# Moving transposes of attention outputs and of late q from the tensor engine to the DMA, with v sorted earlier and k sorted per batch

## The chip, the cores and the metric

One core of one Trainium2 chip. The metric is the device time of one execution in microseconds (us). Executions of one kernel mostly agree within 0.3 to 1%; verdicts compare kernels run alternately on the same chip. A ratio below is the mean time of one kernel's fast runs over that of the other's fast runs of the same rounds, so it is not quite the ratio of the medians that stand beside it. An execution more than 1.5% above the fastest of the same kernel is labelled slow. Spans in a profile are some 2 us shorter than the device time. A profile is of one execution of a kernel, not of the median. To land, for a DMA, is counted from the start of its issue until its data is there.

PE is the tensor engine, ACT the scalar engine, DVE the vector engine, POOL the GpSimd engine, SP the sync engine, which here only issues DMAs.

## The reference

```
P = sort_net; 5 times: softmax over rows, then divide by the column sums     # 4 batches, 8 heads, 8x8
k_sorted = einsum('bhij,bhjcd->bhicd', P, k_b)      # 8 blocks of 96 rows, d = 64; v likewise
attn = softmax(q_b @ k_sb^T / 8) @ v_sb             # inside each block of 96
x = attn, as 3072 tokens x 512
g = s * relu(x @ w_in)^2 + b                        # 512 -> 2048
out = g @ w_out                                     # 2048 -> 512, float32
```

## The kernel before

All work is in eight tiles of 384 tokens; a batch is two tiles. A tile's attention (scores, exp on ACT, product with v, division on DVE) leaves `X[t]` with tokens on partitions. The first dense layer (`ffn1`) needs features on partitions (`XT[t]`), so PE transposes X into PSUM and an engine copies it out. The pieces of later tiles' attention are slotted between the matmuls of the dense layers by queues: q of a batch is transposed by PE, k and v are sorted by PE with block-diagonal matrices `pd1` (batches 0, 1) and `pd2` (batches 2, 3).

```
    def q_piece(b, hp0, eng):                     # q: 24 PE transposes and a copy of 128x1536
        ...
    def k_piece(b, c0, nc2, nb, eng):             # k: nc2 matmuls, 4 copies out of PSUM
        ...
    def v_read(b, eng):                           # sorted v goes to DRAM and is read back,
        ...                                       # 64 values (128 bytes) to a row
            eng.dma_start(out=VS[b][cp * (BLK // 2):(cp + 1) * (BLK // 2), :, 0:D],
                          in_=src.rearrange("g (c two) d -> two c g d", two=2)[cp])
    def t_piece(t, eng, n0=0, nn=HB):             # x: 16 PE transposes and a copy
        ...
    ffn2(1, qu)
    v_read(3, nc.gpsimd)
    load_q(3)
    ...                                           # q and k of batch 2 in the queue
    ffn1(2, qu)
    ffn1(3, qu)
    qu = Queue(attn(4) + attn(5), 24)
    ffn2(2, qu)
    ffn2(3, qu)
```

PSUM buffers are `psa` (3 buffers of two banks, for the first layer and most pieces) and `psb` (2 of one bank, for the second layer). DMAs of one issuing engine are issued in program order; POOL issues the loads and the read-back of sorted v of batches 2 and 3, SP the stores.

The softmax here doesn't subtract the row's maximum and nothing guards it: scores larger than these inputs give would overflow.

## Time and profile before

The median is 249.4 us (248.31 to 249.7 over 4 runs). PE is the bound: 94% busy. The groups of PE work give a timeline by stage (a stage begins with its first dense matmul; a pair of tiles each):

| stage | starts at, us | length, us |
|---|---|---|
| set-up, attention, first layer of tiles 0 and 1 | 0 | 61.9 |
| second layer 0, 1 with attention of 2, 3 | 61.9 | 35.3 |
| first layer 2, 3 with q and k of batch 2 (and k of 3) | 97.2 | 28.8 |
| second layer 2, 3 with attention of 4, 5 | 126.0 | 27.0 |
| first layer 4, 5 (nothing else) | 153.0 | 20.8 |
| second layer 4, 5 with attention of 6, 7 | 173.8 | 28.4 |
| the rest | 202.2 | 45.6 |

The lines behind this table stand in the prediction. Read the fifth row as the pace PE can have, and the third as the place where a first layer costs 8 us more than that.

### The profile page before, as it was taken

To read this page: it belongs to the slowest core of one execution; us is meant where nothing else is said; L and a number is where in the kernel's file an instruction comes from. 1 tells how busy PE (TensorE), PEld (TensorE's weight loads), DVE (VectorE), ACT (ScalarE), POOL (GpSimd) and SP (SyncE) were. 2 spreads that over 40 slices of the span, in tenths; PEclk is the share of its full clock that TensorE was granted. 3 is DMA by queue.
4 is the path that set the end of the run, shared out by engine and by line. 5 is a ranking of instruction groups with operands and counts; after the bars stand their busy time and mean duration, and the time that the engine had idled before them with its cause. 6 is when DMAs were issued, how large, how long until landed. Compare 5 with 4: busy or idle time off the path is not lost.

```text
span 247.8 us, 4978 instructions
## 1 busy us (share of the span) xinstructions
PE 233.1 (94%) x2128; PEld 140.9 (57%) x2128; DVE 133.2 (54%) x260; ACT 116.3 (47%) x156; POOL 39.3 (16%) x51
## 2 busy tenths in 40 slices
PE   8879799799999899998899999999999999999993
PEld 4578699645554456655555555666555566664441
DVE  5776556899992545846675345444353444442221
ACT  6346566335358274477852342666341536661000
POOL 7720200497910027000000000000000000000000
PEclk9955579999999999999999999999999999999999
DMA  5999999999799929991001212000012120001122
GB/s 65 195 194 212 212 205 205 218 204 236 144 99 152 343 90 145 132 173 22 0 4 42 87 43 84 4 0 0 4 42 87 42 87 0 3 0 42 51 76 86
DMA packets 20214, 24.97 MB, mean 101 GB/s; under 512 B 7520, under 2 KB 14432, under 8 KB 19680
## 3 DMA queue, kind: packets, MB, share of 16 engines
q0 software_dynamic: 8400, 15.21, 35.8%
q1 hardware_dynamic: 11792, 9.45, 14.8%
q8 instruction: 16, 0.26, 0.5%
q14 instruction: 6, 0.05, 0.1%
HBM read 29.63 MB, written 8.65 MB: 155 GB/s over the span
## 4 chain that ended last, share of the span: by engine, by line
PE 69%; DVE 12%; DMA 9%; ACT 6%; issue 1%; SPq 0%; DVEq 0%
PE ops L459 29%; PE hps L433 27%; DMA vs<-dv 5%; PE pv L386 4%; DVE gt L438 3%; DMA dv<-vn 3%; ACT rt L437 3%; PE sc L359 3%; PE tr L414 2%; ACT ks L230 2%; PE tv L304 2%; DVE ks L228 2%; DVE qt L228 1%; PE tk L278 1%; DMA sn<-in_sort_net_dram 1%
## 5 line engine op out<-in xcount | busy, mean ns | idle before, releaser
L433 PE MATMUL hps<-xt,wi 128*128 128x384 bf16 (+1 forms) x576 | 89.2, 311 | 2.4 <-ACT ks L230 1.1
L459 PE MATMUL ops<-wo,gt 128*128 128x512 bf16 x384 | 90.5, 380 | 0.0
L433 PEld LDWEIGHTS <-wi 128*128 128x128 bf16 x576 | 54.3, 99 | 31.7 <-issue 4.1
L437 ACT ACTIVATE rt<-hps 128x768 bf16<-128x768 f32 (+1 forms) x72 | 53.2, 739 | 38.1 <-PE hps L433 34.1
L438 DVE TENSOR_TENSOR gt<-rt 128x768 bf16<-128x768 bf16 (+1 forms) x72 | 43.0, 601 | 43.2 <-ACT rt L437 42.8
L459 PEld LDWEIGHTS <-gt 128*128 128x128 bf16 x384 | 35.1, 98 | 38.4 <-issue 0.6
L450 DVE SCALAR_TENSOR_TENSOR ot<-ops,s_bc,bias 128x512 f32<-128x512 f32 x24 | 18.0, 748 | 36.4 <-PE ops L459 36.4
L362 ACT ACTIVATE at<-sc 96x768 bf16<-96x768 f32 x32 | 24.2, 802 | 24.1 <-PE sc L359 24.1
L391 DVE TENSOR_TENSOR x<-pv,rec 96x512 bf16<-96x512 f32 (+1 forms) x36 | 22.6, 628 | 1.3
L230 ACT COPY xt<-tr 128x1536 bf16<-128x1536 bf16 x6 | 8.6, 1438 | 23.6 <-PE tr L414 23.6
L228 DVE CAST ks<-tk 64x512 bf16<-64x512 f32 (+1 forms) x28 | 18.5, 662 | 1.7 <-PE tk L278 1.3
L583 POOL TENSOR_TENSOR csum<-csum,wo 128x512 f32<-128x512 f32 x14 | 17.6, 1255 | 1.0
L230 ACT CAST ks<-tk 64x512 bf16<-64x512 f32 (+1 forms) x24 | 13.9, 580 | 7.2 <-PE tk L278 6.9
L390 DVE RECIPROCAL rec<-pv 96x8 f32<-96x8 f32 (+1 forms) x36 | 7.0, 193 | 17.4 <-PE pv L386 17.4
L386 PEld LDWEIGHTS <-at 96*128 96x128 bf16 (+1 forms) x256 | 11.9, 104 | 5.6 <-DMA vs<-dv 1.5
L386 PE MATMUL pv<-vs,at 96*128 96x66 bf16 (+1 forms) x256 | 12.9, 199 | 1.8 <-DMA vs<-dv 1.0
L359 PEld LDWEIGHTS <-ks 64*96 64x96 bf16 x256 | 8.5, 132 | 6.1 <-issue 5.0
L359 PE MATMUL sc<-qt,ks 64*96 64x96 bf16 x256 | 10.8, 223 | 0.3 <-DVE ks L228 0.2
L172 PE MATMUL wp<-zt 128*128 128x256 bf16 x50 | 9.6, 321 | 1.1 <-DVE warm L104 1.1
L278 PE MATMUL tk<-pd,kb 64*128 64x64 bf16 (+1 forms) x144 | 8.3, 216 | 0.9 <-DVE pd L511 0.9
L278 PEld LDWEIGHTS <-kb 64*128 64x128 bf16 (+1 forms) x144 | 7.4, 106 | 3.0 <-issue 2.2
L228 DVE COPY qt<-tq 128x1536 bf16<-128x1536 bf16 x4 | 7.0, 1754 | 3.5 <-PE tq L259 3.5
(67 smaller groups left out, 116.8 us busy)
## 6 DMA issues: line engine op xcount, KB each, us to landing
out_dram<-ot SPq DMA_DIRECT2D x24, 256.0 KB, 2.0
kb<-in_k_dram POOLq DMA_DIRECT2D x4, 768.0 KB, 21.8
vb<-in_v_dram POOLq DMA_DIRECT2D x4, 768.0 KB, 19.0
qr<-in_q_dram POOLq DMA_DIRECT2D x3, 768.0 KB, 35.4
wi<-in_moe_w_in_dram POOLq DMA_DIRECT2D x2, 1024.0 KB, 19.1
wo<-in_moe_w_out_dram POOLq DMA_DIRECT2D x2, 1024.0 KB, 30.2
dv<-vn SPq DMA_DIRECT2D x6, 256.0 KB, 3.6
vs<-dv POOLq DMA_DIRECT2D x4, 384.0 KB, 11.3
```

Of the source, the lines that this page charges most:

```text
L228: nc.vector.tensor_copy(out=out, in_=in_)
L230: nc.scalar.copy(out=out, in_=in_)
L278: nc.tensor.matmul(out=ps[:, c, :], lhsT=kb[pr, c0 + 2 * c:c0 + 2 * c + 2, :].rearrange("p c d -> p (c d)"), rhs=rhs, start=True, stop=True)
L359: nc.tensor.matmul(out=sc[:, e, n * BLK:(n + 1) * BLK], lhsT=ks[pr, g0 + n, :], rhs=QT[b][pr, hp, q0:q0 + BLK], start=True, stop=True)
L362: nc.scalar.activation(out=at, in_=sc[:, :, 0:TG], func=AF.Exp, scale=scale)
L386: nc.tensor.matmul(out=pv[e][0:m, (n - n0) * VW:(n - n0 + 1) * VW], lhsT=atf[:, c0:c0 + m], rhs=VS[b][:, gi, :], start=True, stop=True)
L391: nc.vector.tensor_tensor(out=x[:, n0:n0 + nn, hp * 128:(hp + 1) * 128].rearrange("p n (e d) -> p e n d", e=2), in0=pvv[:, :, :, 0:D], in1 ...
L433: nc.tensor.matmul(out=hps[:, f, 0:nt], lhsT=wi_at(hp, f0 + f), rhs=xt[:, hp, c0:c0 + nt], start=(hp == 0), stop=(hp == NHP - 1))
L437: nc.scalar.activation(out=rt[:, :, 0:nt], in_=hps[:, :, 0:nt], func=AF.Relu)
L438: nc.vector.tensor_tensor(out=gt[:, f0:f0 + 2, c0:c0 + nt], in0=rt[:, :, 0:nt], in1=rt[:, :, 0:nt], op=ALU.mult)
L450: nc.vector.scalar_tensor_tensor(out=ot, in0=ops, scalar=s_bc, in1=bias, op0=ALU.mult, op1=ALU.add)
L459: nc.tensor.matmul(out=ops, lhsT=gt[:, f, m * 128:(m + 1) * 128], rhs=wo_at(f), start=(f == 0), stop=(f == NF - 1))
```

## The change

It wants PE free of transposes that a DMA can do, frees the copies out of PSUM that went with them, sorts v of batch 1 a stage earlier so that its way through DRAM is over in time, splits the k sort so that each piece is small, and moves the loads of k and q to where the queues reach them.

```diff
-    qtp = ctx.enter_context(tc.tile_pool(name="qtp", bufs=1))
+    qtp = ctx.enter_context(tc.tile_pool(name="qtp", bufs=2))
 ... q of batches 2, 3 loaded as six DMAs of rows of 64 values
+    def q_turn(b):
+        QT[b] = qtp.tile([128, NHP, S], BF, tag="qt", name=f"qt{b}")
+        for t in range(TQ):
+            nc.sync.dma_start(out=QT[b][:, :, t * 128:(t + 1) * 128],
+                              in_=qr[b][:, t].rearrange("p h d -> p (h d)"), transpose=True)
+    def x_turn(t):
+        XT[t] = xtp.tile([128, HB * NHP, BLK], BF, tag="xt", name="xt")
+        nc.sync.dma_start(out=XT[t], in_=X[t].rearrange("p n m -> p (n m)"), transpose=True)
     def T(t):
-        return lambda: t_piece(t, "s")
+        return lambda: x_turn(t)
 ... V1 (v of batch 1) moved from ffn1(1) into ffn1(0); load_k(2), load_q(2) moved from there
 ... to the queue of ffn2(0), with load_k(3)
-                  T(2), P2(3, 0), S2(3, 2), nothing, P2(3, 2), nothing, T(3)], 24)
+                  T(2), P2(3, 0), S2(3, 2), lambda: q_turn(2), P2(3, 2), T(3), nothing], 24)
-    pieces = [lambda: q_piece(2, 0, "v"), lambda: q_piece(2, 2, "v")]
-    for i in range(6):
-        pieces += K2(i * 16, "sv"[i % 2])
-    qu = Queue(pieces + [nothing], 16)
+    qu = Queue([nothing if i % 2 else K(2, i * 8, 8, "vs"[i // 2 % 2]) for i in range(12)]
+               + [nothing] * 4, 16)
     ffn1(2, qu)
     ffn1(3, qu)
+    v_read(3, nc.gpsimd)
+    load_q(3)
 ... K(3) in three pieces in the queue of ffn2(2); q_turn(3) after ffn2(3)
```

The order on SP that this makes: x of tile 2, six transposes of q of batch 2, then x of tile 3.

More of the change, by code (lines that the diff above doesn't have):

```diff
@@ L78, in load_q @@
     def load_q(b, part=slice(0, 128)):
+        if b > 1:
+            qr[b] = qrp.tile([128, TQ, H, D], BF, tag="qr", name=f"qr{b}")
+            for t in range(TQ):
+                nc.gpsimd.dma_start(
+                    out=qr[b][:, t],
+                    in_=q[b][:, t * 128:(t + 1) * 128, :].rearrange("h p d -> p h d"))
+            return
         if b not in qr:
@@ L263, in q_piece @@
              ps[:, :, 0:S].rearrange("q a (t p) -> q a p t", t=TQ), eng)
+    def q_turn(b):
+        QT[b] = qtp.tile([128, NHP, S], BF, tag="qt", name=f"qt{b}")
+        for t in range(TQ):
+            nc.sync.dma_start(out=QT[b][:, :, t * 128:(t + 1) * 128],
+                              in_=qr[b][:, t].rearrange("p h d -> p (h d)"), transpose=True)
     def k_piece(b, c0, nc2, nb, eng):
         pr = brows(b)[1] if nb == 1 else slice(0, 128)
-        rhs = (pd1[pr].rearrange("p e m i -> p (e m i)") if nb == 1
-               else pd2.rearrange("p b e m i -> p (b e m i)"))
+        rhs = (pd1[pr] if b < 2 else pd2[pr, b - 2]).rearrange("p e m i -> p (e m i)")
         if nc2 * nb > 8:
@@ L417, in t_piece, with xt_at @@
         evac(dst, src, eng)
+    def x_turn(t):
+        XT[t] = xtp.tile([128, HB * NHP, BLK], BF, tag="xt", name="xt")
+        nc.sync.dma_start(out=XT[t], in_=X[t].rearrange("p n m -> p (n m)"), transpose=True)
+    def xt_at(t, hp, n0, nn):
+        if t < 2:
+            return XT[t][:, hp, n0 * BLK:(n0 + nn) * BLK]
+        return XT[t].rearrange("p (n a) t -> p a n t", a=NHP)[:, hp, n0:n0 + nn, :]
     GT = {}
@@ L426, in ffn1 @@
             GT[t] = gtp.tile([128, NF, TG], BF, tag="gt", name="gt")
-        gt, xt = GT[t], XT[t]
+        gt = GT[t]
         c0, nt = n0 * BLK, nn * BLK
@@ L433, in ffn1 @@
                     nc.tensor.matmul(out=hps[:, f, 0:nt], lhsT=wi_at(hp, f0 + f),
-                                     rhs=xt[:, hp, c0:c0 + nt],
+                                     rhs=xt_at(t, hp, n0, nn),
                                      start=(hp == 0), stop=(hp == NHP - 1))
@@ L551 @@
     load_v(*brows(2))
-    load_k(*brows(2))
-    load_q(2)
     def P(t, hp, *r):
@@ L566 @@
                    lambda: t_piece(0, "v", 2, 2), SC(1, 3), P(1, 0)], 8), 0, 2)
-    ffn1(0, Queue([nothing, P(1, 1), nothing, P(1, 2), nothing, P(1, 3), nothing,
+    ffn1(0, Queue([V1(0), P(1, 1), V1(1), P(1, 2), V1(2), P(1, 3), V1(3),
                    lambda: t_piece(1, "v")], 8), 2, 2)
-    build_pd2()
-    V1(0)()
-    V1(1)()
+    V1(4)()
+    V1(5)()
     csum = const.tile([128, d_model], FP)
@@ L585 @@
     csums(0, 8)
-    ffn1(1, Queue([V1(i) for i in range(2, 6)] + [lambda: v_read(1, nc.sync)] + [nothing] * 3, 8))
+    v_read(1, nc.sync)
+    ffn1(1, Queue([nothing] * 4 + [build_pd2] + [nothing] * 3, 8))
     load_v(*brows(3))
@@ L592, with K @@
                + [lambda c0=c0: k_piece(1, c0, 16, 1, "vsv"[c0 // 32])() for c0 in range(0, BLK, 32)]
-               + [bias_piece, S2(2, 0), V2[0], S2(2, 2), V2[1], V2[2], V2[3],
+               + [seq(lambda: load_k(*brows(2)), lambda: load_k(*brows(3)), lambda: load_q(2), bias_piece), S2(2, 0), V2[0], S2(2, 2), V2[1], V2[2], V2[3],
                   P2(2, 0), V2[4], P2(2, 2), seq(V2[5], lambda: v_read(2, nc.gpsimd)), S2(3, 0),
-                  T(2), P2(3, 0), S2(3, 2), nothing, P2(3, 2), nothing, T(3)], 24)
+                  T(2), P2(3, 0), S2(3, 2), lambda: q_turn(2), P2(3, 2), T(3), nothing], 24)
     ffn2(0, qu)
-    load_k(*brows(3))
     ffn2(1, qu)
+    def K(b, c0, nc2, eng):
+        return lambda: k_piece(b, c0, nc2, 1, eng)()
+    qu = Queue([nothing if i % 2 else K(2, i * 8, 8, "vs"[i // 2 % 2]) for i in range(12)]
+               + [nothing] * 4, 16)
+    ffn1(2, qu)
+    ffn1(3, qu)
     v_read(3, nc.gpsimd)
     load_q(3)
-    rest = []
-    def K2(c0, eng):
-        return [lambda: rest.append(k_piece(2, c0, 8, 2, eng)), lambda: rest.pop()()]
-    pieces = [lambda: q_piece(2, 0, "v"), lambda: q_piece(2, 2, "v")]
-    for i in range(6):
-        pieces += K2(i * 16, "sv"[i % 2])
-    qu = Queue(pieces + [nothing], 16)
-    ffn1(2, qu)
-    ffn1(3, qu)
-    qu = Queue(attn(4) + attn(5), 24)
+    at4, at5 = attn(4), attn(5)
+    for i, n in enumerate((1, 4, 6)):
+        at4[n] = K(3, 32 * i, 16, "vsv"[i])
+    qu = Queue(at4 + at5, 24)
     ffn2(2, qu)
     ffn2(3, qu)
+    q_turn(3)
     ffn1(4)
     ffn1(5)
-    qu = Queue([lambda: q_piece(3, 0, "s"), lambda: q_piece(3, 2, "v")]
-               + attn(6) + attn(7), 24)
+    qu = Queue(attn(6) + attn(7), 24)
     ffn2(4, qu)
```

## The prediction

> **What bounds the kernel now.** I read the first part of the page first, for the busiest engine, then the summary of the chain that ended last, then a table of busy time by stage, and last the waits of the tensor engine (PE).
>
> ```profile
> PE 233.1 (94%) x2128; PEld 140.9 (57%) x2128; DVE 133.2 (54%) x260; ACT 116.3 (47%) x156; POOL 39.3 (16%) x51
> PE 69%; DVE 12%; DMA 9%; ACT 6%; issue 1%; SPq 0%; DVEq 0%
> ```
>
> PE is busy 94% of a span of 247.8 us, and 69% of the last-ending chain is its work. A busy PE is not a PE at its peak, so the stages decide. I cut the span where the matmul groups change (columns: window and length, then busy time of PE, weight loads, DVE, ACT, POOL, clock, DMA share, GB/s):
>
> ```profile
> 46.20:61.90 15.70, 14.13 (x96) 7.72 (x95) 14.29 (x20) 6.16 (x8) 13.29 (x13) 1.00 1.10 216
> 61.90:97.20 35.30, 34.22 (x366) 18.35 (x365) 21.86 (x36) 18.09 (x21) 11.32 (x10) 1.00 0.86 158
> 97.20:126.00 28.80, 26.39 (x230) 16.82 (x228) 18.22 (x28) 20.11 (x28) 1.67 (x2) 1.00 0.59 86
> 126.00:153.00 27.00, 26.77 (x257) 14.35 (x256) 13.62 (x27) 8.26 (x10) 0.00 (x0) 1.00 0.14 50
> 153.00:173.80 20.80, 20.80 (x133) 12.55 (x130) 8.33 (x16) 13.49 (x16) 0.00 (x0) 1.00 0.04 13
> 173.80:202.20 28.40, 28.40 (x306) 15.49 (x304) 13.34 (x25) 9.60 (x11) 0.00 (x0) 1.00 0.13 48
> ```
>
> The fifth line is a pure first dense layer of two tiles (tiles 4 and 5): 128 matmuls in 20.80 us, the full pace of this kernel (1.30 us per slot of 8). The third line is the same layer for tiles 2 and 3 with the q and k work of batch 2 in it: 28.80 us, with PE idle 2.4 us and slowed beside that. From 126 us on, PE streams: whatever is taken from PE there comes off the time one for one.
>
> In the chain in order of time (start, us, what) I looked for places where it leaves PE:
>
> ```profile
> 101.45 1.67 DVE qt L228
> 103.64 1.68 DVE qt L228
> 108.29 0.59 ACT ks L230
> 115.51 0.58 ACT ks L230
> ```
>
> These are copies out of PSUM for q and k of batch 2, which hold up the three PSUM buffers that the dense layer needs too.
>
> **What the Trainium skill says.** "VectorE: DVE Perf Modes", section "The three transpose paths": a TensorE transpose ends in PSUM, the DMA crossbar one in SBUF; for one 128x128 block it gives 390 ns against 1309 ns. The trace agrees on the first: every transposed tile is followed by a copy (1438 ns on ACT for xt, 1754 ns on DVE for qt). A block's PE cost is less here: 16 transposes of a tile took 0.68 us in the chain.
> "DMA: Bandwidth & Descriptors", "Latency and other measured facts": an effective 261 GB/s for a DMA transpose with a non-contiguous middle dimension. The kernel before has no such DMA, so no run here shows it yet. Same page, "Issuing engines are not separate DMA queues": all DMAs share the 16 engines. The trace agrees: from 93 to 112 us, with the sorted v of two batches and q of batch 3 together, their landings took 9.2 to 15.9 us, where the out tiles later take 2.0 us.
> "SBUF — State Buffer", "Who interferes with whom": a DVE instruction with two SBUF inputs contends with a GpSimd instruction that reads SBUF. The trace agrees: the squaring (gt) takes 0.56 us in the later dense layers, and four in a row took 5.20 us at 59.71 us, under the csum additions of POOL.
>
> **The change part by part.** The compiled orders of the two kernels give the counts: transposes of x 128 to 32, of q 240 to 144, k sorting matmuls 144 to 192; dense and attention matmuls are the same.
>
> 1. x of tiles 2 to 7 turned by DMA. Off PE: 6 x 0.68 = 4.1 us, two tiles in each of the stretches at 62, 126 and 174 us. Off ACT: 6 x 1.44 = 8.6 us, which mostly lay beside PE work. Added: six transposing DMAs on the SP queue of 96 x 2048 x 2 bytes = 393 KB. At the skill's 261 GB/s that is an estimate of 1.5 us of movement each; with issue and completion I allow 4 to 8 us. Tiles 2, 4 and 6 are turned 8 us or more before their dense layer, and tiles 5 and 7 have 10.4 us (the other tile's dense layer).
> 2. q of batches 2 and 3 turned by DMA: off PE 4 x 0.79 = 3.2 us (two pieces at 97 us, two at 174 us), off DVE 3 x 1.75, off ACT 1.44 us. Added: 12 transposing DMAs of 131 KB (an estimate of 0.5 us movement at that rate, perhaps 1.5 us each in issue), and q loads in rows of 64 values instead of 384.
> 3. k of batches 2 and 3 apart: 48 matmuls of 128 columns become 96 of 64. In the first sort 32 of the narrow kind take 1.88 us in the chain, 0.059 us each, and the wide ones cost about the same (8 in 0.47 to 0.61 us). So 48 more cost 2.8 us of PE. They go to the dense stretch at 97 us (batch 2: the same 48 x 0.059 as before, but half the evacuation) and to the second layer of tiles 2 and 3 (batch 3: +2.8 us).
> 4. v of batch 1 sorted one stage earlier. In the first dense layer DVE then has, per pair of slots, 2 squarings (2 x 0.34), a normalisation (0.20 + 0.69) and a new evacuation (0.68): 2.2 us, against PE's 6.8/4 + 0.33 = 2.0. So that stretch gets about 1.4 us longer by DVE. In return the stretch from 46.2 to 61.9 loses its sorts and its 1.6 us of idle PE and needs about 12.8 us: -2.9. Sum -1.5 us. The round trip of sorted v through DRAM now ends early, so the one wait of PE for it (1.0 us at 82 us) goes.
>
> By stretch, in us:
> - start to 61.9: -1.5 (part 4).
> - 61.9 to 97.2: -1.4 (two x transposes) -1.0 (the wait for v) = -2.4.
> - 97.2 to 126: before 28.8. After: 20.8 of dense layer plus 48 x 0.059 = 2.8, and 0.2 for rests, 23.8. The evacuations of one k piece shrink to 4 x 0.42 or 0.45 = 1.8 us every other slot of 1.3 and go through the PSUM pool that the first layer leaves empty, so I expect no waits: -5.0.
> - 126 to 153: -1.4 (x) -0.5 (scores waited for k evacuations) +2.8 (k of batch 3) +1.1 (my working of the PSUM ring: a k piece on DVE takes 4 x 0.70 = 2.8 us ahead of the normalisations, and the next scores need those buffers) = +2.0.
> - 174 to 202: -1.4 (x) -1.6 (q) = -3.0.
> Sum -9.9 us. I give back 0.9 us on average for a late transpose (below): -9.0, so 249.7 - 9.0 = **240.7 us**.
>
> **The rivals.**
> - **SP becomes a queue that blocks.** It issues in program order. The transposes of q of batch 2 wait there for q's loads, which now start only after csum has left POOL (68.4 us in the trace before) behind two k loads. Full-size loads run at some 205 GB/s early on, 3.8 us for 0.79 MB; rows of 128 bytes, as the sorted v has, move at perhaps half that. So q should land at 86 to 92 us, and its transposes are due at about 90. Six of them at 1.7 us make 100 us, then x of tile 3 some 6 us: 106, against its need at 105 us. So a stall of PE of 0 to 3 us ahead of the second tile's dense layer is quite likely, and more if a transpose is slow: at 4 us each it is 15 us. For: many DMAs in flight then. Against: there is slack of a whole dense layer. Time then 241 to 255 us.
> - **The crossbar is slow.** If each x tile took its 12 blocks at 1309 ns one after the other, 15.7 us, tiles 5 and 7 would be 5 to 8 us late each, out tiles would wait behind q of batch 3, and the result would be 255 us or more. Against: the skill's bandwidth figure, and that a DMA is spread over 16 engines. I give this about 1 in 10.
> - **The expected gain at 97 us is smaller**, since four evacuations in a row delay ACT's relu there too; DVE and ACT stay under 1.3 us per slot on average, so I expect at most 1.5 us of loss: 242 us.
> - **More gain than summed**: the first dense layer does not slow, the k pieces at 126 us do not stall: 238 us.
>
> **Range and chances.** From 236.5 (all transfers hidden, no new stall) to 247.0 us (stall of SP of some 5 us, and little won at 97 us). 2% is 5.0 us; the gains of parts 1 and 2 on a streaming PE alone, less the k matmuls, are 4.5 us, so faster by over 2% needs the stretch at 97 us or the early part as well. I put 0.78 on faster, 0.14 on same, 0.08 on slower.
>
> **What would show it.** PE's busy sum should fall by about 5 to 7 us, with 4 us in transposes of x. The stretch of tiles 2 and 3 should be near 24 us with hardly a wait of the dense matmuls for ks copies. The two last second-layer stretches should be 29 and 25.4 us. In the DMA issues the x transposes should land within 8 us; the waits of PE should hold no large entry for xt or qt. Wrong would show as: a wait of hps for a DMA of xt (at about 105 us for tile 3, or at half of each later dense stretch), DVE waiting on ot buffers because SP is held, or a longer first dense layer that eats part 4.

## The result, and the profile after

The changed kernel takes 260.65 us (median of 4, 258.98 to 261.8) against 249.43; ratio 1.045 (95% interval 1.039 to 1.052). Slower, where 240.7 was predicted.

From the page of the changed kernel, the busy times and the chain by engine:

```profile
PE 227.0 (88%) x1964; PEld 134.5 (52%) x1984; DVE 129.0 (50%) x265; ACT 106.5 (41%) x153; POOL 47.9 (19%) x61
PE 70%; DVE 10%; DMA 7%; SPq 6%; issue 3%; ACT 2%; DVEq 0%
```

PE's busy time fell by 6.1 us, as wanted, and the span grew by 10.8. A busy sum says nothing about the end: PE idles elsewhere. SPq in the chain, 0% before and 6% now, is SP's own issuing. The stages of the changed kernel, with the columns explained in the prediction:

```profile
60.80:93.80 33.00, 32.33 (x328) 17.06 (x333) 22.00 (x35) 16.65 (x20) 13.40 (x15) 1.00 1.37 199
93.80:138.20 44.40, 25.77 (x176) 14.42 (x177) 13.78 (x28) 16.19 (x27) 10.20 (x10) 0.77 1.04 90
138.20:166.70 28.50, 27.12 (x269) 14.38 (x273) 16.95 (x32) 9.25 (x13) 0.00 (x0) 1.00 0.21 61
187.70:212.70 25.00, 24.78 (x220) 12.82 (x223) 11.14 (x23) 6.77 (x9) 0.00 (x0) 1.00 0.24 69
```

One stage went wrong, the first layer of tiles 2 and 3: 44.4 us (with 0.5 us of waiting for x of tile 2 at its start) with PE busy 25.8 and a mean granted clock of 0.77. Its PE timeline (start, length, line; in brackets the idle time before, and what ended it; `hps` is the first layer, `tk` the sorting of k):

```profile
105.14 1.48 PE L458 MATMUL hps<-xt,wi 128*128 128x384 bf16 x8
124.78 2.74 PE L458 MATMUL hps<-xt,wi 128*128 128x384 bf16 x8 [18.16 <-DMA xt<-x]
127.45 0.60 PE L293 MATMUL tk<-pd,kb 64*128 64x64 bf16 x8
127.99 3.44 PE L458 MATMUL hps<-xt,wi 128*128 128x384 bf16 x16
```

PE waits 18.16 us for the transposed x of tile 3. And after the idle time it is slow for a while: 8 matmuls take 2.74 us, not 1.48 (the granted clock reads 0.50 from 111 to 129 us). The excess of the three groups over their usual 1.48, 0.40 and 2.77 us is 2.1 us. SP's timeline shows where x of tile 3 stood:

```profile
86.42 2.93 SPq L437 DMA_TRANSPOSE xt<-x  x1
91.05 16.16 SPq L278 DMA_TRANSPOSE qt<-qr  x6
107.31 10.21 SPq L437 DMA_TRANSPOSE xt<-x  x1
```

Here the second column is issuing, not transfer. In the chain of waits, five of the six q transposes issue in 1.2 to 1.6 us and the sixth in 8.77. But the last three landed only after 20.8 to 22.0 us, so they too were slow, and not only the one whose issue was. Then x of tile 3 takes 10.21 us to issue and lands 17.4 us after it began, at 124.7. The same instruction for tiles 4 to 7 issues in 1.4 to 1.5 us and lands in 3.9 to 4.0. What POOL had just issued beside it (start, length, line):

```profile
93.36 5.35 POOL L360 DMA_DIRECT2D vs<-dv  x4 [18.26 <-DMA dv<-vn]
98.69 2.68 POOL L84 DMA_DIRECT2D qr<-in_q_dram  x3
```

These are the read-backs of sorted v of batches 2 and 3 (four DMAs, landing 10.7 to 19.7 us after issue) and the first loads of q of batch 3.

**Theory:** transposing DMAs that run beside the read-backs and q loads are several times slower, and x of tile 3 stood in SP's order behind six of them. Two causes are in this: A, the order; B, the slowness of a single transpose beside those loads. **Rivals:** the transposes are slow by themselves in that place (too many in flight), or the q loads alone do it.

The traces already say one thing more: the slowness is not special to transposes. In the kernel before, which has none by DMA, two plain stores of out (256 KB each) stood on SP in that same stretch, issued from 93.56 us on. From its answers about DMAs (the two alone, then all 24 with the median; the last figure is us to landing):

```profile
out_dram<-ot SPq DMA_DIRECT2D x1, 256.0 KB, 6.9
out_dram<-ot SPq DMA_DIRECT2D x1, 256.0 KB, 11.9
out_dram<-ot SPq DMA_DIRECT2D x24, 256.0 KB, 2.0
```

### The profile page after: what moved, and what is told of

It is laid out like the page before. It is cut to its first block, busy times and chain, and to the rows that moved or that the text cites. A ratio compares the mean times of both kernels' runs of the same rounds, so it can differ in the third digit from the quotient of the medians.

```text
span 258.6 us, 4722 instructions
## 1 busy us (share of the span) xinstructions
PE 227.0 (88%) x1964; PEld 134.5 (52%) x1984; DVE 129.0 (50%) x265; ACT 106.5 (41%) x153; POOL 47.9 (19%) x61
## 4 chain that ended last, share of the span: by engine, by line
PE 70%; DVE 10%; DMA 7%; SPq 6%; issue 3%; ACT 2%; DVEq 0%
PE ops L484 29%; PE hps L458 28%; DMA xt<-x 7%; SPq L278 6%; PE sc L374 3%; PE pv L401 3%; PE tk L293 2%; DVE x L406 2%; PE tv L319 2%; DVE ks L237 1%; ACT ks L239 1%; PE tv L349 1%; DVE gt L463 1%; DVE ot L475 1%; DVE vn L237 1%
## 5 line engine op out<-in xcount | busy, mean ns | idle before, releaser
L458 PE MATMUL hps<-xt,wi 128*128 128x384 bf16 (+1 forms) x576 | 91.3, 316 | 19.7 <-DMA xt<-x 18.7
L484 PE MATMUL ops<-wo,gt 128*128 128x512 bf16 x364 | 87.2, 379 | 1.3 <-issue 0.3
L463 DVE TENSOR_TENSOR gt<-rt 128x768 bf16<-128x768 bf16 (+1 forms) x72 | 42.0, 585 | 63.7 <-ACT rt L462 63.5
L484 PEld LDWEIGHTS <-gt 128*128 128x128 bf16 x384 | 35.3, 98 | 38.8 <-issue 0.6
L237 DVE CAST ks<-tk 64x512 bf16<-64x512 f32 (+1 forms) x36 | 20.9, 579 | 4.8 <-PE tk L293 4.3
L239 ACT CAST ks<-tk 64x256 bf16<-64x256 f32 (+1 forms) x28 | 13.7, 489 | 8.7 <-PE tk L293 8.4
L84 POOL DMA_DIRECT2D qr<-in_q_dram x12 | 10.6, 908 | 9.9 <-DMA vs<-dv 6.9
L405 DVE RECIPROCAL rec<-pv 96x8 f32<-96x8 f32 (+1 forms) x36 | 6.9, 193 | 10.7 <-PE pv L401 10.7
L374 PE MATMUL sc<-qt,ks 64*96 64x96 bf16 x256 | 10.8, 223 | 1.0 <-DVE x L406 1.0
L293 PEld LDWEIGHTS <-kb 64*128 64x128 bf16 x192 | 7.6, 104 | 5.7 <-issue 5.6
L293 PE MATMUL tk<-pd,kb 64*128 64x64 bf16 x192 | 9.2, 204 | 0.9 <-DVE pd L536 0.9
L360 POOL DMA_DIRECT2D vs<-dv x4 | 5.3, 1349 | 18.3 <-DMA dv<-vn 18.3
## 6 DMA issues: line engine op xcount, KB each, us to landing
kb<-in_k_dram POOLq DMA_DIRECT2D x4, 768.0 KB, 10.2
vb<-in_v_dram POOLq DMA_DIRECT2D x4, 768.0 KB, 19.3
vs<-dv POOLq DMA_DIRECT2D x4, 384.0 KB, 18.8
```

The source lines that it names most:

```text
L237: nc.vector.tensor_copy(out=out, in_=in_)
L293: nc.tensor.matmul(out=ps[:, c, :], lhsT=kb[pr, c0 + 2 * c:c0 + 2 * c + 2, :].rearrange("p c d -> p (c d)"), rhs=rhs, start=True, stop=True)
L374: nc.tensor.matmul(out=sc[:, e, n * BLK:(n + 1) * BLK], lhsT=ks[pr, g0 + n, :], rhs=QT[b][pr, hp, q0:q0 + BLK], start=True, stop=True)
L458: nc.tensor.matmul(out=hps[:, f, 0:nt], lhsT=wi_at(hp, f0 + f), rhs=xt_at(t, hp, n0, nn), start=(hp == 0), stop=(hp == NHP - 1))
L463: nc.vector.tensor_tensor(out=gt[:, f0:f0 + 2, c0:c0 + nt], in0=rt[:, :, 0:nt], in1=rt[:, :, 0:nt], op=ALU.mult)
L484: nc.tensor.matmul(out=ops, lhsT=gt[:, f, m * 128:(m + 1) * 128], rhs=wo_at(f), start=(f == 0), stop=(f == NF - 1))
```

## The experiments

Twelve kernels ran, all correct. The kernel before was at 248.8 to 249.7 us in the same rounds.

### x of tile 3 ahead of q

```diff
-                  ..., lambda: q_turn(2), P2(3, 2), T(3), nothing], 24)
+                  ..., nothing, P2(3, 2), T(3), lambda: q_turn(2)], 24)
```

> Only the order on the SP queue changes: x of tile 3 is turned ahead of the six q transposes of batch 2, not behind them. Theory A (order: x of tile 3 stood behind 16 us of q transposes that were slowed by the Pool queue's loads): x of tile 3 is issued at about 93.5 us, lands within 8 us, no wait of PE near 107 us, time 240 us +- 2. Rival B (a crossbar transpose that runs beside the 128-byte-row loads is itself some 17 us, whatever stands ahead of it): x of tile 3, issued at 93.5 beside the same loads, lands only at about 108 to 111 us; PE still waits 2 to 5 us, time 243 to 246 us.

Measured: 242.72 us median (three fast runs 241.81 to 242.77, one of 245.9), ratio 0.973 (0.969 to 0.978). The profile is of the 245.9 run, which is slow. In it x of tile 3, issued at 93.83 us, landed in 7.0 us, in time; PE's wait of 18 us is gone. But the six q transposes now took SP this long, and the scores of tile 4 waited 2.6 us for q:

```profile
96.73 23.17 SPq L278 DMA_TRANSPOSE qt<-qr  x6
```

So the order decides who pays (A); in the profiled run the q transposes were still slow. Whether the three fast runs had that wait too, no profile shows.

### Loads held until x of tile 3 has landed

```diff
+    def hold():                      # a copy on POOL that has to wait for XT[3]
+        nc.gpsimd.tensor_copy(out=gate2, in_=XT[3][0:1, 0, 0:1])
-    ... seq(V2[5], lambda: v_read(2, nc.gpsimd)) ..., T(3), nothing], 24)
+    ... V2[5] ..., T(3), seq(hold, lambda: v_read(2, nc.gpsimd))], 24)
```

Since POOL issues in order, sorted v of batch 3 and q of batch 3 wait too.

> SP order as in the change, but sorted v of batches 2 and 3 and q of batch 3 are held on the Pool queue until x of tile 3 has landed, so nothing of that queue is in flight beside the transposes. If contention makes the transposes slow (common to A and B): six q transposes issue in about 1.3 us each, x of tile 3 is issued at about 99.5 and lands at about 104, PE waits under 1 us, time 240 us +- 2. If the transposes were slow for another reason (their source tiles, their own number in flight): the last q transpose still takes over 8 us and PE still waits over 10 us, time above 250 us.

Measured: 240.76 us, ratio 0.969 (0.963 to 0.975). SP's order is that of the change, and its timeline now reads:

```profile
91.23 8.74 SPq L278 DMA_TRANSPOSE qt<-qr  x6
100.07 1.45 SPq L437 DMA_TRANSPOSE xt<-x  x1
```

8.74 us for six q transposes, not 16.16; 1.45 us for x of tile 3, not 10.21, and it landed in 3.8. So taking the traffic away cures it, and the rival "slow by themselves" falls. The remaining wait for xt is 1.2 us, at tile 2, whose turn (8.5 us to land) runs beside the loads of q of batch 2. The stage that was 44.4 us is 23.5:

```profile
95.10:118.60 23.50, 23.48 (x177) 13.77 (x178) 13.07 (x27) 16.20 (x27) 10.87 (x11) 1.00 0.85 116
118.60:147.00 28.40, 27.44 (x273) 14.31 (x272) 16.92 (x32) 9.25 (x13) 0.00 (x0) 1.00 0.97 100
```

### Only q of batch 3 held

```diff
     v_read(3, nc.gpsimd)
+    hold()
     load_q(3)
```

> Only the loads of q of batch 3 (rows of 64 values) are held until x of tile 3 has landed; sorted v of batches 2 and 3 still flows. If the q loads are what slows the transposes: time 240 to 245 us, PE's wait at 107 us under 5 us. If the sorted v is: PE's wait stays at 10 us or more, time 252 to 259 us.

Measured: 256.69 us median, but two of the four runs, 257.58 and 256.76, are slow; the fast ones are 252.88 and 256.62 (ratio 1.023, 1.012 to 1.033), so the time is only roughly known. All four are above every run of the kernel before in these rounds (up to 250.47). In the profile, of the 257.58 run, the six q transposes took SP 24.86 us and PE waited 13.9 us for x of tile 3. This is what was forecast if sorted v is to blame: the q loads are not needed for the effect.

### q of batch 2 back on PE

```diff
-        if b > 1:                    # rows of 64 values
+        if b > 2:
-    ..., lambda: q_turn(2), P2(3, 2), T(3), nothing], 24)
+    ..., nothing, P2(3, 2), T(3), nothing], 24)
-               + [nothing] * 4, 16)
+               + [lambda: q_piece(2, 0, "v"), nothing, lambda: q_piece(2, 2, "s"), nothing], 16)
```

> q of batch 2 goes back to PE transposes (as before the change, in the first layer of tile 3) with its old load of long rows; x of tiles 2 to 7 and q of batch 3 stay with the DMA. Theory A: x of tile 3 is issued at 93.5 us and lands in time, PE pays 1.6 us for q and perhaps 1 us for the evacuations, time 241 to 244 us. Rival B: x of tile 3 lands at 108 to 111 us as in the run with x first, time 245 to 248 us.

Measured: 241.03, 241.69 and 242.8 us in three runs, as theory A has it, and 255.1 in the fourth, which is the profiled one. Its wait of PE:

```profile
PE hps L458 <- DMA xt<-x: 13.1, 1, 13.1
```

There x of tile 3 was issued at 93.2 us with no q transpose ahead of it, 2 us after the read-backs had begun, and took 25.3 us to land. So B does happen: in this execution a transpose behind no other was that late. A plain store of out issued after it took as long (24.4 us). This is a single run; it is a reason to prefer holding the loads to reordering.

### The read-backs on ACT's queue

```diff
-    ... seq(V2[5], lambda: v_read(2, nc.gpsimd)) ..., T(3), nothing], 24)
+    ... V2[5] ..., T(3), seq(lambda: v_read(2, nc.scalar), lambda: v_read(3, nc.scalar))], 24)
+    hold()                           # q of batch 3 held, as above
```

> As the run that held only q of batch 3, but the two read-backs of sorted v are issued on the ACT queue and not on the Pool queue, at the end of the second layer of tile 1. Same bytes, same rows, same time, another queue. Theory A1 (the packets that the Pool queue forms are what the transposes stand behind): q transposes issue in about 1.3 us each, x of tile 3 lands before 107 us, PE's wait for it under 2 us, time 240 to 245 us (ACT loses a few us to issuing). Theory A2 (any 128-byte-row read-back beside a transpose slows it): the last q transpose still takes over 8 us, PE waits 8 us or more, time above 250 us.

Measured: 255.78 us, ratio 1.027 (1.023 to 1.031), slower. Neither forecast was met as a whole: the q transposes were nearly as quick as A1 has it, but x of tile 3 was not and the time was A2's, for a reason that neither named. The six q transposes took SP 9.65 us, x of tile 3 took 5.59 to issue and 10.0 to land: faster than beside the POOL queue. But PE's waits show a new blocker:

```profile
PE hps L458 <- ACT rt L462: 12.2, 1, 12.2
```

ACT's program stood still in issuing four DMAs, from 92.11 for 19.26 us, and its relu with it. So the issuing of plain DMAs was held up too, beside transposes. As this also spread the read-backs over a longer time, it stays open whether the form of the POOL queue's packets matters.

### x of tiles 4 to 7 alone, in the kernel before

```diff
-        return lambda: t_piece(t, "s")
+        return lambda: (x_turn(t) if t >= 4 else t_piece(t, "s"))
```

> The kernel before with one part: x of tiles 4 to 7 turned by DMA, where no load is in flight. If a transpose taken off a streaming PE comes off the time one for one, 4 x 0.68 = 2.7 us less, 246.3 us, and the transposes land in 4 us. If it hides (something else bounds these stretches): 248.5 to 249.5 us.

Measured: 246.99 us against 248.8 (medians), ratio 0.991 (0.988 to 0.994): about 2.2 us less by the ratio, 1.8 by the medians, clear of noise though within the 2% that counts as the same. The landings were 3.9 to 5.6 us, and the two stages that lost two transposes each read:

```profile
125.20:150.70 25.50, 25.06 (x220) 12.96 (x224) 12.98 (x25) 6.77 (x9) 0.00 (x0) 1.00 0.29 68
171.70:198.50 26.80, 26.43 (x266) 14.06 (x271) 12.61 (x24) 8.22 (x10) 0.00 (x0) 1.00 0.22 65
```

25.5 and 26.8 us against 27.0 and 28.4. Where no load runs, a transpose taken off a streaming PE does come off the time; the summed 2.7 us lie inside the interval (1.4 to 3.0 us).

### Loads held, v of batch 1 sorted late

```diff
-    ffn1(0, Queue([V1(0), P(1, 1), V1(1), ...], 8), 2, 2)
+    ffn1(0, Queue([nothing, P(1, 1), nothing, ...], 8), 2, 2)    # and V1, build_pd2 as before the change
```

> The held-loads kernel with part 4 undone (v of batch 1 sorted after the first dense layer of tile 0, as before). By the prediction's sum part 4 is worth 1.5 us plus the wait of 1.0 us for sorted v: 243.2 us against 240.8. If the first dense layer gives all of it back, or the wait for sorted v is gone anyway since the loads are out of its way: 240.5 to 241.5 us.

Measured: 242.99 us, ratio 0.976 (0.973 to 0.979), against 0.969 (0.963 to 0.975) with v early. The intervals touch; the medians differ by 2.2 us, the spans by 2.5. Of these, 1.2 us lie ahead of the second layer, which begins at 62.2 us, not 61.0; the other 1.3 are PE's wait for x of tile 2, 2.5 us here and 1.2 there. That wait varies between executions of the same code so far (2.1 and 2.4 us in the two runs with a disturbance below), so only the 1.2 us are surely the earlier sort's. The wait for sorted v, which the prediction also booked on it, is gone here too, but that says little: it is also absent from the profile of the run before this one, whose code up to there is the kernel before's. It comes and goes between executions.

### Loads held, k of batches 2 and 3 together

```diff
-    qu = Queue([nothing if i % 2 else K(2, i * 8, 8, "vs"[i // 2 % 2]) ...
+    pieces = [nothing] * 2
+    for i in range(6):
+        pieces += K2(i * 16, "sv"[i % 2])                        # as before the change, without q
-        at4[n] = K(3, 32 * i, 16, "vsv"[i])
```

> The held-loads kernel with k of batches 2 and 3 sorted together again, as before (48 wide matmuls and 24 evacuations of 64x512 in the first layer of tiles 2 and 3, through the PSUM pool of that layer). If the separate k pieces pay: the first-layer stretch of tiles 2 and 3 gets 3 us or more longer than it gains in the second layer, time above 242 us. If only the q copies were the trouble there: the second layer of tiles 2 and 3 is 2.8 + 1.0 us shorter, the first layer 1 to 2 us longer, time 238.5 to 240 us.

Measured: 239.55 us, ratio 0.963 (0.960 to 0.967). The two stages concerned:

```profile
93.50:120.10 26.60, 24.45 (x176) 15.50 (x178) 15.62 (x27) 18.78 (x27) 10.81 (x11) 1.00 0.84 111
120.10:145.20 25.10, 24.87 (x220) 12.90 (x224) 12.38 (x26) 6.83 (x9) 0.00 (x0) 1.00 1.06 104
```

26.6 + 25.1 = 51.7 us, against 23.5 + 28.4 = 51.9 with k apart. Splitting k moved 3 us from one stage to the next and gained nothing. The forecast for "only the q copies" had the time right, and the first layer 1 to 2 us longer, where it was 3.1. With q off PE, the joint sort no longer costs what it did at 28.8 us.

### A version meant to beat both

```diff
+    qu = Queue([lambda c0=c0: k_piece(2, c0, 4, 2, "sv")() for c0 in range(0, BLK, 8)], 16)
```

On the kernel of the section above: joint k in 12 small pieces through `psb`, each half copied out by another engine; x of tile 2 turned a slot earlier.

> A version meant to beat both kernels: loads held, k of batches 2 and 3 sorted together, but in pieces of 4 matmuls through the PSUM pool that the first layer leaves empty, the two halves of each piece evacuated on two engines; x of tile 2 turned one slot earlier. Against the joint-k run (its first layer of tiles 2 and 3 took 26.6 us by its PE groups, with 2.1 us of waits on ACT in it): if those waits came from the shared PSUM buffers, the stretch takes 24 to 25 us and the time is 237 us; if ACT and DVE are themselves full there (ACT 23.3 us of work by its durations), it stays at 26 us and 239.5 us.

Measured: 239.03 us, ratio 0.957 (0.952 to 0.962). The first layer of tiles 2 and 3 took 24.4 us, and PE's waits for ACT in it are gone, as forecast if the shared PSUM buffers had been the cause; but the pieces were also smaller and their copies spread over two engines, and no run separates these. (ACT itself was not full: the joint-k line above has it busy 18.8 of 26.6 us, not the expected 23.3.) The time forecast with it, 237 us, was missed: of the 2.2 us won, 1.1 went to the turn of x of tile 2, which landed in 9.4 us and kept PE waiting 1.7 us (0.6 in the joint-k profile), and 0.8 to a wait of the next layer for a copy of k.

### A read-back beside x of tile 5

This and the next run start from the held-loads kernel and put the suspected traffic where nothing else loads.

```diff
+    def beside():                    # POOL waits for the last of X[5]
+        nc.gpsimd.tensor_copy(out=gate3, in_=X[5][0:1, HB - 1, d_model - 1:d_model])
+        for _ in range(2): ...       # read sorted v of batch 3 back into VS[3] again
+    at5[6] = beside
```

> The held-loads kernel with one disturbance added where no load runs: just ahead of the turn of x of tile 5 the sorted v of batch 3 is read back twice more (same bytes, same place, 128-byte rows, Pool queue). In the undisturbed kernel x of tile 5 lands in 3.9 us and the six q transposes of batch 3 in 2.4 us each. If the read-back is the cause: x of tile 5 takes over 8 us to land, or the q transposes over 8 us; the time stays within 2 us unless x of tile 5 is later than its slack of 10.4 us. If the cause lay in the earlier stretch (its q loads, its stores): landings stay within 1.5 us of undisturbed.

Measured: 248.1 us; ratio 0.993 (0.987 to 1.000), the same as the kernel before, against 0.969 without the disturbance. x of tile 5 landed in 14.1 us, not 4.0; PE waited 5.0 us for it, up to 163.2 us, and then took 12.19 us for that tile's 64 matmuls, where those of tile 4 had taken 10.56:

```profile
147.64 10.56 PE L458 MATMUL hps<-xt,wi 128*128 128x384 bf16 x64
163.21 12.19 PE L458 MATMUL hps<-xt,wi 128*128 128x384 bf16 x64 [5.00 <-DMA xt<-x]
```

The six q transposes of batch 3 took SP this long, against 8.82 us undisturbed:

```profile
151.29 17.45 SPq L278 DMA_TRANSPOSE qt<-qr  x6
```

The cause can be put in at will, at a place where nothing else of the old stage is. The plain store of out just ahead of x of tile 5 took 6.4 us to land.

### Loads of long rows beside x of tile 5

```diff
+    def beside():
+        nc.gpsimd.tensor_copy(out=gate3, in_=X[5][0:1, HB - 1, d_model - 1:d_model])
+        load_k(*brows(2))
+        load_k(*brows(3))
```

> As the run before, but the disturbance is two loads of k (rows of 24 KB in DRAM, 0.79 MB each landed, same Pool queue; the values are not used). If it is the short rows of the read-back that hurt: x of tile 5 lands within 6 us and the q transposes within 5 us. If any load on the Pool queue hurts as much: landings over 8 us as in the other run.

Measured: 243.91 us, ratio 0.980 (0.974 to 0.986), unclear at 2%. The profile is of the slowest of the four runs, 246.08 us. x of tile 5 took 7.07 us to issue and 11.8 to land, and PE waited 2.7 us for it:

```profile
151.06 7.07 SPq L437 DMA_TRANSPOSE xt<-x  x1
158.23 10.60 SPq L278 DMA_TRANSPOSE qt<-qr  x6
```

The loads were issued from 149.27 us on and landed in 9.2; the first q transpose behind landed in 5.5 us, the others in 2.5 to 3.7. The plain store issued just ahead, at 150.6, took 10.8. So short rows are not required. My reading, which no run tests further, is that a DMA of SP beside any bulk load of the POOL queue runs at a fraction of its pace until that load is done; the read-backs may hurt more because they are under way longer (in the run before, POOL issued them from 147.2 to 164.0 us).

### x of tile 2 on PE

```diff
-        return lambda: x_turn(t)
+        return lambda: (x_turn(t) if t > 2 else t_piece(t, "s"))
```

On the version meant to beat both.

> The version of before last (loads held, joint k in small pieces) with x of tile 2 turned by PE again, since its DMA turn stands beside the q loads and stores of that stage (9.4 us to land, PE waited 1.7 us). PE pays 0.68 us and loses the wait: 238 us if the wait was all that it cost; unchanged at 239 us if the copy out of PSUM (1.44 us on ACT) makes the dense layer wait as long.

Measured: 237.24 us (236.78 to 237.48), ratio 0.950 (0.948 to 0.952), the best. No wait of PE for a transposed x or q is left in its profile.

## Why the prediction was wrong

Stage by stage, in us (the 0.5 us of waiting for x of tile 2 in the changed kernel counts to the stage ahead of it here):

| stage | before | predicted | changed | loads held |
|---|---|---|---|---|
| to the second layer of tile 0 | 61.9 | 60.4 | 60.8 | 61.0 |
| second layer 0, 1 | 35.3 | 32.9 | 33.5 | 34.1 |
| first layer 2, 3 | 28.8 | 23.8 | 43.9 | 23.5 |
| second layer 2, 3 | 27.0 | 29.0 | 28.5 | 28.4 |
| first layer 4, 5 | 20.8 | 20.8 | 21.0 | 20.8 |
| second layer 4, 5 | 28.4 | 25.4 | 25.0 | 25.3 |
| the rest | 45.6 | 45.6 | 45.9 | 45.8 |
| span | 247.8 | 237.9 | 258.6 | 238.9 |

**The step that failed** is the term of the sum "I give back 0.9 us on average for a late transpose", and under it the landing of x of tile 3 at 106 us. It measured 18.7 us of waits for transposed x (18.2 of them for tile 3), and 2.1 us more of PE at a low granted clock behind the wait. 260.65 - 18.7 - 2.1 = 239.9 us is what the rest of the sum came to, within 1 us of its 240.7.

**Why it was mis-sized.** The prediction named the place: SP in program order, q of batch 2 ahead of x of tile 3, "106, against its need at 105 us". Up to the start of q it was right: q of batch 2 landed from 84.5 to some 92 us, about as worked out, no transpose waited for it, and the six began at 91.05. But its central figures were 1.7 us for a q transpose and "some 6 us" for x. Undisturbed, both were generous: 1.5 us of issue for a q transpose (six in 8.82 us), 3.9 us to landing for an x. Beside the read-backs the six took 16.2 us, where 10.2 were worked out, and x took 17.4. What it left out of these figures is that its own quotation on shared DMA engines applied to these very instructions: the trace before showed read-backs and loads of q from 91 to 112 us, exactly where the change puts seven transposes, and stores of SP landing there in 6.9 and 11.9 us. It did write "at 4 us each it is 15 us", near what came, but as a tail of the rival, worth little in the 0.9 us of the sum. The rival that it held for 1 in 10, a slow crossbar, is also not what happened: alone the crossbar was fast.

**Part 1** (x by DMA). Right where nothing else loads: 2.2 us for four tiles, where 4 x 0.68 = 2.7 was summed. "8 us or more before their dense layer" was wrong for tile 2: its turn was issued at 86.42 us for a need at 93.76 and landed in 7.8, and in the held-loads kernels PE waited 0.6 to 2.5 us for it. In the stage at 62 us it seems to gain nothing for tile 2: putting that one back on PE made the best version, with an interval that just touches the one before.

**Part 2** (q by DMA). Right on PE and DVE: 25.0 us for the second layer of tiles 4 and 5 against 25.4 predicted. The q transposes of batch 2 were what x of tile 3 stood behind.

**Part 3** (k apart). The sizes by stage were right, 23.5 us for the first layer with the loads held against 23.8, 28.5 us against 29.0 for the next stage, and also the new wait of the scores for PSUM buffers (1.0 us where 1.1 was worked out). But it credited the whole gain of the 28.8 us stage to the change as it stands; the joint-k run shows that the two stages together are no better for the split. Of the 5.3 us won in that stage, 3.1 only moved to the next; the other 2.2 are there with joint k too, where q's transposes (1.6 us of PE by the prediction's figures) and their copies are gone. No run separates transposes from copies.

**Part 4** (v early). The first dense layer's second half grew from 6.8 to 8.2 us, the size given, but not "by DVE": DVE was busy 7.3 of these 8.2 us and PE all of them, with no wait, at the 2.0 us per pair of slots that the prediction had for PE (its 2.2 for DVE would have made 8.8). The net of 1.5 us was 1.1 in this trace. The wait of 1.0 us for sorted v went, but it can be absent in the old order too, as the run with x of tiles 4 to 7 alone shows.

**The rivals' times.** "SP becomes a queue that blocks" had 241 to 255 us and was the right mechanism with too small a size. The range's upper end of 247.0 us stood on a stall of "some 5 us".

What stays open: at which level a transpose (or a store) and a load get in each other's way (packets, queues or the crossbar). The runs show that the loads cause it, that holding them back removes the wait for x of tile 3, and that the same read-backs from another queue slowed the q transposes less, under another timing.

## What to carry to other kernels

Before moving work to a DMA, list what else the DMA engines carry between its issue and its need, and size the transfer by that, not by its undisturbed time; how the stores of the old kernel fare in that stretch (11.9 us against 2.0 here) is a warning that costs no run. In a queue that issues in order, put the transfer that is needed first ahead, and hold bulk loads whose need is far away until it has landed: a one-element copy that reads its destination is enough of a gate. And test a bundle by its parts: here x of four tiles gained 2.2 us alone, v early 1.2 us and k apart nothing (both with the loads held; q by DMA was not tried alone), and the fault of one transfer hid all of it.

## What the Trainium skill lacked or had wrong

- "DMA: Bandwidth & Descriptors", "Rules for kernel authors": "A transpose next to ordinary DMAs needs nothing". That held for the values (all runs were correct), but the time is lacking: a transpose of 393 KB landed in 3.9 us alone, 11.8 beside two k loads, 14.1 beside read-backs of 128-byte rows, and 17.4 in the changed kernel. A plain store of 256 KB went from 2.0 to 11.9 us in the kernel before.
- The same page, "Issuing engines are not separate DMA queues": issuing time is said to be usually small beside the DMA. Here a transpose held SP's program for 10.2 us, and four read-backs beside transposes held ACT's for 19.3 us and stopped its relu for PE (12.2 us). What a held issue does to the issuing engine's own work is lacking there.
- The 261 GB/s that the prediction took for movement is a rate, and no time for one transfer follows from it: 393 KB in 3.9 us from issue to landing is 101 GB/s, and 131 KB in 2.4 us is 55 GB/s, undisturbed and with issue and completion included (an estimate from these two: some 1.7 us fixed, and 175 GB/s for the rest). No page gives a time for one transpose of such a size.
